# One more block by seven products in the last batch, and other PSUM banks for the last whole chunk's output

## The chip, the cores and the metric

The kernel runs on one core of a Trainium2 chip. The metric is the device time of one execution in microseconds (us), the median of several runs. The engines of the core have a queue of instructions each and run them strictly in their queue's order: TensorE (PE in the profile, with its weight loads as PEld), VectorE (DVE), ScalarE (ACT), GpSimd (POOL) and SyncE (SP, which issues DMAs). They wait for each other through semaphores. Matmuls write into PSUM, which holds eight banks of 128 partitions x 512 float32; VectorE and ScalarE read it from there.

## What is computed

For each of four batches, a cross-covariance attention over channels, then a multiplicative feed-forward network over all tokens:

```python
B, N, C = (4, 5824, 256)
qn = q / (np.linalg.norm(q, axis=1, keepdims=True) + 1e-06)
kn = k / (np.linalg.norm(k, axis=1, keepdims=True) + 1e-06)
s = kn.transpose(0, 2, 1) @ qn / tau
...
a = np.exp(s)
a /= a.sum(-1, keepdims=True) + 1e-09
x = v @ a                    # 23296 tokens x 256
a = x @ w1                   # w1, w2: 256 x 1024
b = x @ w2
h = a * b @ w3               # 1024 x 1024
return h @ w_out             # 1024 x 256
```

All inputs and the output are float32; the kernel multiplies in bfloat16 and adds up in float32.

## The kernel before

**What is multiplied.** The kernel never forms x. For each batch it folds the attention matrix into w1 and w2 (`Wf`), so that a and b come straight from v transposed (`vT`), and it multiplies w3 by w_out once (`W_sb`). A batch has 5824 tokens: eleven whole chunks of 512 (c = 0 to 10) and a small one of 192 columns (c = 11, 128 tokens and 64 left over). Each chunk has eight blocks of 128 hidden units (j = 0 to 7). For a block (c, j), `normal` (L988) runs two matmuls of 512 columns into a bank for a, ScalarE casts it to bf16 (`as`, L985), two more go into another bank for b, and VectorE multiplies the two into the staging tile `abh` (L1017, or L1013 into `left` for the small chunk).

**Blocks by seven.** In the last batch (b = 3) some blocks of two neighbouring chunks c and c + 1 are made together by a scheme of Strassen's kind, `by_seven` (L1028): seven matmuls of 512 columns in place of eight, on sums of tokens (`tsum`, made by POOL) and sums of weights (`wsum`). Its banks are X, Y, Z and T. The first X product is copied to Y by ScalarE (L1040), T is copied to SBUF (`t`, L1046), VectorE adds X and t into Z (L1051), X and t into `bs` (L1070), and makes the two products `abh` (L1075, L1082); ScalarE casts Y to `as`. X is used for four products, and the fourth waits until bs has been read from the third. So against two plain blocks, seven products cost ScalarE three copies in place of two, and VectorE four instructions in place of two. `BY_SEVEN` (L554) says how many blocks of each pair of chunks are made so; `plan` (L1387) spreads them evenly over the eight j by the formula (2 i + 1) 8 // (2 k) and places them among the plain ones. Up to two blocks by seven are under way at once, and their steps are mixed with those of plain blocks.

**Output.** When a chunk is whole, its output is made from `abh` and `W_sb`, mixed in between the blocks of later chunks. Most chunks go by `seven_products` (L758): products of 128 x 128 into prodA (bank out0), prodB and prodC (bank out1), on sums that POOL makes (`S`, L790 and L792, 2.1 us each) or, for chunks 4 and 6 of the last batch, by four accumulating DMAs that POOL issues (L800). Chunks 0, 2 and 9 of the last batch go plainly by `emit_half` (L1088): 32 matmuls of 256 columns, the first half into out0, the second into out1, each copied to the staging tile `osb` and stored from SP. Chunk 10, the last whole one, and the small chunk 11 go block by block as their blocks are made: `single` (L896) tells the planner when, and `emit_out` (L1117) issues the matmuls, 4 x 8 of 256 columns for chunk 10 into out0 and out1, 2 x 8 for chunk 11 into the banks G and out2. The last two blocks of chunk 11 are issued at the very end (`ends`).

**Banks.** Eight tags stand for the eight banks: ab0 to ab3, out0, out1 (which have one use at a time), G and out2. G and out2 hold scores and norms of the next batch while there is one. In the last batch (`spare`) they join ab0 to ab3 as a ring of six for the a, b, X, Y, Z and T tiles (`rings`, L575). A tag in the set `held` is not given out.

**What sets the order.** The kernel's order is written out by a planner that runs when the program is built: `now` and `free` keep estimated times of the engines and banks, and `step` (L1418) picks among the plain line, up to two lines by seven, and the output line the one that can go first by its estimate (the lambda that each line yields). POOL's sums are put in by `pool_due` by due times, and loads of v, q and k at moments of an agenda; ahead of each load, `gate` (L955) makes POOL copy one element of the last-made `abh` tile, so that POOL, which issues the load, waits for that instruction of VectorE. So a change to the blocks moves estimates, and with them the order on every engine, from the first block it touches on.

Of the kernel before, what the change touches and what calls it, by code (L numbers as in the profile page):

```python
# [32 lines left out]
def kernel(  # L33
# [14 lines left out]
    B, N, C = q.shape  # L48
# [16 lines left out]
    NCH = NT // 4 + 1  # L65
# [485 lines left out]
        )  # L551


    BY_SEVEN = {(3, 0): 3, (3, 2): 5, (3, 4): 4, (3, 6): 5, (3, 8): 4}  # L554
    PAIRED = {b: tuple(c for b2, c in sorted(BY_SEVEN) if b2 == b) for b in range(B)}
    PLAIN = {0: (0, ), 1: (), 2: (), 3: (0, 2, 9, )}
    BY_DMA = {3: (4, 6, )}
# [7 lines left out]
    FAR = 1e9  # L565
    base = [0.0]
    free = {}
    held = set()

    def work_on(engine, cost, *after):  # L570

        now[engine] = max(now[engine], *after, 0.0) + cost
        return now[engine] + LATE[engine]
# [146 lines left out]
    w_made = [FAR]  # L720
# [34 lines left out]
    def out_bank(tag, ready=0.0):  # L755
        return max(free.get(tag, 0.0), ready)
# [133 lines left out]
    def plain_products(b, c, ab2, whole):  # L890

        for i in range(FT):
            yield lambda i=i: max(out_bank(f"out{i // 4}", whole), w_made[0])
            emit_half(b, c, i, ab2)

    def single(b, c, j, ab, ready):  # L896

        yield lambda: max(
            ready, w_made[0], out_bank("out0"), out_bank("out1"), 0.0 if queued.get(b, 0) == NCH - 1 - b // (B - 1) else FAR
        )  # L900
        emit_out(b, c, j, ab)

# [12 lines left out]
    queued = {}  # L915
# [72 lines left out]
    def normal(b, c, j):  # L988
# [32 lines left out]
        if c == NCH - 1 and b == B - 1 and j >= FT - LAG_END:  # L1021
            ends.append(lambda only=None: emit_out(b, c, j, ab, only))
        elif c == NCH - 1 or (b == B - 1 and c == NCH - 2):
            put_out(b, c, single(b, c, j, ab, ready), 1)
# [63 lines left out]
    def emit_half(b, c, i, ab2):  # L1088

        h, jj = divmod(i, 4)  # L1090
        if i % 4 == 0:
            out_tiles[b, c, h] = psum.tile([P, 2, D], F32, tag=f"out{h}", name=f"o_{b}_{c}_{h}", bufs=1)
        if i == 0:
            out_tiles[b, c] = work.tile([P, 4, D], F32, tag="o_sb", name=f"osb_{b}_{c}", bufs=3)
        t, o = out_tiles[b, c, h], out_tiles[b, c]
        for j in (2 * jj, 2 * jj + 1):
            for k in range(2):
                nc.tensor.matmul(  # L1098
                    t[:, k, :], lhsT=ab2[j // 4][:, h, j % 4, k * P : (k + 1) * P], rhs=W_sb[:, j, :],
                    start=(j == 0 and k == 0), stop=(j == FT - 1), skip_group_check=True,  # L1100
                )
        work_on("PE", 4 * (D * MM_COL + MM_FIX))
        read = now["PE"] + LATE["PE"]
        if i == 3:
            nc.scalar.copy(o[:, 0:2, :], t)
            free["out0"] = work_on("ACT", 0.475, read)
        elif i == FT - 1:
            if b == B - 1:
                nc.scalar.copy(o[:, 2:4, :], t)
                free["out1"] = work_on("ACT", 0.475, read)  # L1110
            else:
                nc.vector.tensor_copy(o[:, 2:4, :], t)
                free["out1"] = work_on("DVE", 0.6, read)
            rows = out[b * N : b * N + NT * P, :].rearrange("(p i) c -> p i c", i=NT)
            nc.sync.dma_start(out=rows[:, 4 * c : 4 * c + 4, :], in_=o)

    def emit_out(b, c, j, ab, only=None):  # L1117

        small = c == NCH - 1
        if small:  # L1120
            lhs = [ab[:, :P]]
            if b % 2 == 1:
                lhs.append(lefts[b // 2][:, j, :, :].rearrange("p b t -> p (b t)")[:, P : P + 2 * LEFT])
        else:
            lhs = [ab[:, i // 2, i % 2 * P : (i % 2 + 1) * P] for i in range(4)]
        if j == 0:
            out_tiles[b, c] = [
                psum.tile([P, 2, D], F32, tag=tag, name=f"o_{b}_{c}_{tag}", bufs=1)
                for tag in ((("G", "out2") if b == B - 1 else ("out0", "out1"))[: len(lhs)] if small else ("out0", "out1"))
            ]  # L1130
        tl = out_tiles[b, c]
        for s, lhsT in reversed(list(enumerate(lhs))) if small and b == B - 1 else enumerate(lhs):
            if only is not None and s != only:
                continue
            h, o = (s, 0) if small else divmod(s, 2)
            nc.tensor.matmul(  # L1136
                tl[h][:, o, :], lhsT=lhsT, rhs=W_sb[:, j, :],
                start=(j == 0 and o == 0), stop=(j == FT - 1 and (small or o == 1)),
                skip_group_check=True,
            )  # L1140
        work_on("PE", len(lhs) * (D * MM_COL + MM_FIX))
        if j == FT - 1:
            read = now["PE"] + LATE["PE"]
            free["out0"] = work_on("ACT", 0.475, read)
            free["out1"] = work_on("DVE", 0.6, read)
            o = work.tile([P, 4, D], F32, tag="o_sb", name=f"osb_{b}_{c}", bufs=3)
            rows = out[b * N : b * N + NT * P, :].rearrange("(p i) c -> p i c", i=NT)
            if small:
                if b % 2 == 1 and only != 0:
                    o2 = work.tile([P, D], F32, tag="kr", name=f"oleft_{b}", bufs=1)  # L1150
                    nc.vector.tensor_copy(o2, tl[1][:, 0, :])
                    for m in (b - 1, b):
                        k = (m - b + 1) * LEFT
                        store = lambda m=m, k=k, queue=nc.sync: queue.dma_start(
                            out=out[m * N + NT * P : (m + 1) * N, :], in_=o2[k : k + LEFT, :]
                        )
                        if m < B - 1:
                            store()
                        else:
                            last_rows.append(store)  # L1160
                if only != 1:
                    nc.scalar.copy(o[:, 0, :], tl[0][:, 0, :])
                    other = nc.scalar if b == B - 1 else nc.sync
                    other.dma_start(out=rows[:, NT - 1, :], in_=o[:, 0, :])
                    if last_rows:
                        last_rows.pop()(queue=nc.scalar)
            else:
                nc.scalar.copy(o[:, 0:2, :], tl[0])
                nc.vector.tensor_copy(o[:, 2:4, :], tl[1])
                nc.sync.dma_start(out=rows[:, 4 * c : 4 * c + 4, :], in_=o)  # L1170
            if only is None:
                del out_tiles[b, c]
# [214 lines left out]
    def plan(b):  # L1387
# [6 lines left out]
        while c < NCH:  # L1394
            if c in PAIRED.get(b, ()):
                k = BY_SEVEN[b, c]
                mine = [(2 * i + 1) * FT // (2 * k) for i in range(k)]
# [119 lines left out]
```

## Time and profile before

| what | value |
|---|---|
| median of 3 runs | 550.82 us (550.64 to 550.88) |
| the profiled execution | 551.17 us |
| its span, first to last instruction | 549.1 us |
| granted TensorE clock, mean | 0.999 |
| DVE busy in the span | 425.0 us |
| ACT busy | 397.0 us |
| POOL busy | 416.1 us |
| a and b matmuls of 512 columns (L995) | 620 each, 184.4 us each |
| X matmuls on token sums (L980, two of a block's four) | 42, for 21 blocks |

The span is what the profile covers; about 2 us of the execution's time lie around it. The page names an instruction by its source line, engine, operation and tiles, written out<-in, and gives how many there are, their busy time and the mean duration. [...] Batch 3 takes the part of the span from about 436 us to the end: chunks 4 and 5 are made from about 463 to 481 us, chunks 6 and 7 to about 500, and chunk 10's output starts at 539.1.

In the timeline, a bracket behind a row gives how long the engine was idle before it and what ended that; in the chain of waits, "issue" is time in which an engine waited for nothing that the profile shows.

### The profile page before, as it was taken

How to read it: one execution, taken by the hardware profiler on the slowest of the kernel's cores; microseconds unless marked ns; L12 is line 12 of the kernel's file. 1: busy time of each engine (PE TensorE's matmuls, PEld its weight loads, DVE VectorE, ACT ScalarE, POOL GpSimd, SP SyncE). 2: the span in 40 equal slices, each digit the busy share in tenths (PEclk: the TensorE clock that was granted, in tenths of full speed). 3: DMA queues.
4: the chain of work that ended last, by engine and by line, in shares of the span. 5: the costliest groups of instructions: out<-in, count | busy, mean ns of one | idle time of the engine just before them, and what ended most of it. 6: DMA issues, size and time to landing. Idle time of an engine off the chain costs nothing.

```text
span 549.1 us, 12260 instructions
## 1 busy us (share of the span) xinstructions
PE 537.4 (98%) x4608; PEld 350.8 (64%) x4608; DVE 425.0 (77%) x748; ACT 397.0 (72%) x825; POOL 416.1 (76%) x343
## 2 busy tenths in 40 slices
PE   7799999999999999999999999999999999999996
PEld 4564566666677666666658666666667656666675
DVE  5477748999876888888766788888778788889861
ACT  5446648889777788888666888888778667677762
POOL 4270794979999499998996498979999846978560
PEclk9999999999999999999999999999999999999999
DMA  9999987995876849775582857776651334565513
GB/s 214 212 202 208 214 159 154 226 189 108 124 163 147 191 87 195 162 158 125 116 180 88 166 126 153 151 146 119 154 116 78 78 92 110 136 168 135 144 58 128
DMA packets 76747, 80.75 MB, mean 147 GB/s; under 512 B 54416, under 2 KB 59024, under 8 KB 76688
## 3 DMA queue, kind: packets, MB, share of 16 engines
q0 software_dynamic: 16816, 41.03, 42.7%
q1 hardware_dynamic: 59504, 38.22, 25.0%
q8 instruction: 36, 0.59, 0.4%
q10 hardware_dynamic: 368, 0.72, 0.4%
q14 instruction: 23, 0.19, 0.1%
HBM read 78.91 MB, written 23.86 MB: 187 GB/s over the span
## 4 chain that ended last, share of the span: by engine, by line
PE 92%; DMA 5%; DVE 1%; ACT 1%; issue 1%; POOL 0%; ACTq 0%; DVEq 0%; POOLq 0%
PE b L995 25%; PE a L995 25%; PE prodA L830 13%; PE prodC L830 6%; PE G L216 5%; PE prodB L830 3%; PE X L980 3%; DMA k<-in_k_dram 3%; PE o L1098 2%; PE fold L449 2%; DMA q<-in_q_dram 2%; PE o_out L1136 1%; PE w L1285 1%; PE Z L980 1%; PE Y L980 1%; PE T L980 1%
## 5 line engine op out<-in xcount | busy, mean ns | idle before, releaser
L1017 DVE TENSOR_TENSOR abh<-as,b 128x512 bf16<-128x512 bf16 x310 | 211.6, 684 | 68.7 <-ACT as L985 45.0
L985 ACT CAST as<-a 128x512 bf16<-128x512 f32 (+1 forms) x342 | 192.1, 563 | 70.0 <-PE a L995 57.4
L995 PE MATMUL a<-vT,Wf 128*128 128x512 bf16 x620 | 184.4, 379 | 0.1
L995 PE MATMUL b<-vT,Wf 128*128 128x512 bf16 x620 | 184.4, 379 | 0.0
L995 PEld LDWEIGHTS <-Wf 128*128 128x128 bf16 x1368 | 123.1, 98 | 77.7 <-issue 0.7
L790 POOL TENSOR_TENSOR S<-abh,abh 128x1024 bf16<-128x1024 bf16 x37 | 78.8, 2130 | 52.9 <-DVE abh L1017 34.7
L830 PEld LDWEIGHTS <-S 128*128 128x128 bf16 x1216 | 80.1, 98 | 22.9
L230 DVE TENSOR_TENSOR acc<-acc,sq 128x512 f32<-128x512 f32 x132 | 91.6, 694 | 1.2 <-ACT sq L213 0.3
L792 POOL TENSOR_TENSOR S<-S,abh 128x1024 bf16<-128x1024 bf16 x37 | 78.7, 2128 | 2.7
L792 POOL TENSOR_TENSOR S<-abh,S 128x1024 bf16<-128x1024 bf16 x37 | 79.4, 2147 | 0.1
L792 POOL TENSOR_TENSOR S<-abh 128x1024 bf16<-128x1024 bf16 x37 | 78.8, 2131 | 0.1
L830 PEld LDWEIGHTS <-abh 128*128 128x128 bf16 x968 | 64.1, 98 | 20.6 <-issue 0.8
L843 ACT COPY osb<-prodA 128x256 f32<-128x256 f32 x113 | 42.2, 373 | 16.3 <-PE prodA L830 15.7
L216 PE MATMUL G<-k,q 128*128 128x256 bf16 x276 | 52.4, 273 | 0.0
L216 PEld LDWEIGHTS <-q 128*128 128x128 bf16 x276 | 27.0, 98 | 32.1
L830 PE MATMUL prodA<-comb_T,S 128*128 128x128 bf16 x608 | 46.3, 219 | 0.0
L213 ACT ACTIVATE sq<-q 128x512 f32<-128x512 bf16 x69 | 43.8, 635 | 0.0
L213 ACT ACTIVATE sq<-k 128x512 f32<-128x512 bf16 x69 | 43.5, 630 | 0.0
L850 DVE TENSOR_TENSOR osb<-osb,prodC 128x256 f32<-128x256 f32 x76 | 31.4, 414 | 4.4 <-ACT osb L843 3.5
L130 POOL DMA_DIRECT2D q<-in_q_dram x27 | 15.2, 563 | 11.8 <-DMA q<-in_q_dram 5.7
L830 PE MATMUL prodB<-W_sb,abh 128*128 128x128 bf16 x312 | 23.8, 219 | 0.1
L830 PE MATMUL prodA<-W_sb,abh 128*128 128x128 bf16 x312 | 23.8, 219 | 0.0
(176 smaller groups left out, 642.9 us busy)
## 6 DMA issues: line engine op xcount, KB each, us to landing
out_dram<-osb SPq DMA_DIRECT2D x44, 512.0 KB, 3.4
k<-in_k_dram POOLq DMA_DIRECT2D x19, 512.0 KB, 8.0
v<-in_v_dram POOLq DMA_DIRECT2D x19, 512.0 KB, 6.9
q<-in_q_dram POOLq DMA_DIRECT2D x18, 512.0 KB, 5.5
w<-in_moe_w_dram POOLq DMA_DIRECT2D x4, 512.0 KB, 16.6
k<-in_k_dram POOLq DMA_DIRECT2D x4, 320.0 KB, 7.8
v<-in_v_dram POOLq DMA_DIRECT2D x4, 320.0 KB, 4.2
S<-abh SPq DMA_DIRECT2D x4, 256.0 KB, 3.0
```

The costliest lines, as they stand in the source:

```text
L213: nc.scalar.activation(out=sqs[0][:, :, part, :], in_=src[:, o : o + 2, :], func=AF.Square)
L216: nc.tensor.matmul(G[:, ct, :], lhsT=qt[:, i, ct * P : (ct + 1) * P], rhs=kt[:, i, :], start=(pr == 0 and part == 0 and ct == 0), stop=(pr ...
L230: nc.vector.tensor_add(accs[n], accs[n], sqs[0][:, part - 2])
L790: nc.gpsimd.tensor_add(x, a21, a22)
L792: nc.gpsimd.tensor_sub(x, *{2: (sums[1], a11), 3: (a11, a21)}.get(i) or (a12, sums[2]))
L830: nc.tensor.matmul(st[nm][:, i, :], lhsT=a[:, j, i * P : (i + 1) * P], rhs=w[j], start=(first and j == 0 and i == 0), stop=(j == 3), skip_ ...
L843: nc.scalar.copy(quarter(r, d), st[nm])
L850: nc.vector.tensor_add(quarter(r, d), quarter(r, d), st[nm])
L980: nc.tensor.matmul(dst, lhsT=lhsT, rhs=rhs, start=start, stop=True, skip_group_check=True)
L985: nc.scalar.copy(a_sb[:, :n], t[:, :n])
L995: nc.tensor.matmul(t[:, :n], lhsT=Wf[b][:, ct, w, j * P : (j + 1) * P], rhs=rhs_of(b, c, ct), start=(ct == 0), stop=(ct == CT - 1),)
L1017: nc.vector.tensor_mul(ab, two_halves(a_sb), two_halves(t))
```

## The change

```diff
-    BY_SEVEN = {(3, 0): 3, (3, 2): 5, (3, 4): 4, (3, 6): 5, (3, 8): 4}
+    BY_SEVEN = {(3, 0): 3, (3, 2): 5, (3, 4): 5, (3, 6): 5, (3, 8): 4}
...
+    def out_tags(b, c):
+        return ("G", "out2") if (b, c) == (B - 1, NCH - 2) else ("out0", "out1")
+
     def single(b, c, j, ab, ready):

         yield lambda: max(
-            ready, w_made[0], out_bank("out0"), out_bank("out1"), 0.0 if queued.get(b, 0) == NCH - 1 - b // (B - 1) else FAR
+            ready, w_made[0], *(out_bank(t) for t in out_tags(b, c)), 0.0 if queued.get(b, 0) == NCH - 1 - b // (B - 1) else FAR
         )
...
         if j == 0:
+            if b == B - 1 and not small:
+                held.update(("G", "out2"))
             out_tiles[b, c] = [
                 psum.tile([P, 2, D], F32, tag=tag, name=f"o_{b}_{c}_{tag}", bufs=1)
-                for tag in ((("G", "out2") if b == B - 1 else ("out0", "out1"))[: len(lhs)] if small else ("out0", "out1"))
+                for tag in out_tags(b, c)[: len(lhs) if small else 2]
             ]
```

The first edit makes five blocks of chunks 4 and 5 of the last batch by seven products in place of four: j = 0, 2, 4, 5 and 7, where it was 1, 3, 5 and 7. The second lets chunk 10's output of the last batch add up in G and out2, and the small chunk 11's in out0 and out1; from chunk 10's first output matmul on, G and out2 are held back from the ring. The planner's estimate for chunk 10's output looks at the new banks.

In the order of instructions that the changed program is built with, everything up to the last blocks of chunks 2 and 3 of the last batch (some 462 us into the span) is as before. In chunks 4 and 5 the blocks and the pieces of output among them are mixed in another order; some pieces of output of chunks 3 and 5 trade places with their neighbours; from the middle of chunks 6 and 7 on the order is the old one again up to the end of chunk 9's output. There, chunk 10's 32 output matmuls now come ahead of the pair a, b of block (11, 7), the last one, where they came behind it, and on ScalarE and VectorE the two copies of chunk 10's output come ahead of that block's cast and product. On POOL one instruction differs: the gate ahead of the load of v's last piece (chunks 10 and 11) copies from chunk 5's `abh` in place of chunk 4's, and waits for the product of the plain block (5, 6).

## The prediction

> **What bounds the kernel now.** I read the page first: PE is busy 98% of the span, and the chain that ended last is 92% PE. The clock row of its slices stays at full speed.
>
> ```profile
> span 549.1 us, 12260 instructions
> PE 537.4 (98%) x4608; PEld 350.8 (64%) x4608; DVE 425.0 (77%) x748; ACT 397.0 (72%) x825; POOL 416.1 (76%) x343
> PE 92%; DMA 5%; DVE 1%; ACT 1%; issue 1%; POOL 0%; ACTq 0%; DVEq 0%; POOLq 0%
> PEclk9999999999999999999999999999999999999999
> ```
>
> So in the steady part a matmul taken away shortens the program by its own length, unless another engine cannot follow. Next I read the timeline of the last batch, and looked on PE for starts that lie further apart than the width explains. A 512-column matmul follows the one before after 0.22 us, a 256-column one after 0.11. From 458 us on, PE waits noticeably at four places only: 487.1 (0.05 us), 498.4 (0.07), 515.4 (0.29) and 539.2 (0.29). The last is the one that the second edit touches, and the chain of waits shows it:
>
> ```profile
> 537.22 1.76 PE o L1098 x16
> 539.00 0.59 ACT osb L1109
> 539.59 0.04 issue
> 539.64 3.54 PE o_out L1136 x31
> ```
>
> PE finishes chunk 9 (L1098), runs the pair a, b of block (11, 7), starts chunk 10's output in bank out0, and then stands still until ScalarE has copied chunk 9's second half out of bank out1. The stages around the other edit come from the view of windows (columns: window, its length, then busy time and count of PE, PEld, DVE, ACT, POOL, then clock, DMA share, GB/s). Chunks 4 and 5 fill the first, with four blocks by seven; chunks 6 and 7 the second, with five:
>
> ```profile
> 466.00:482.00 16.00, 16.00 (x116) 9.73 (x114) 13.75 (x23) 11.12 (x22) 14.53 (x15) 1.00 0.59 149
> 482.00:499.00 17.00, 17.00 (x152) 10.55 (x150) 15.28 (x27) 12.75 (x29) 12.97 (x10) 1.00 0.63 134
> ```
>
> VectorE is the closest rival of PE: 86% busy with four blocks, 90% with five.
>
> **Part 1, one more block by seven.** Eight matmuls of 512 columns (a and b for two chunks, two halves each) become seven. That takes one matmul from PE, 0.22 us, and the rest of PE's list keeps its length. ScalarE gets one 512-wide copy more (three in place of two, 0.59 us each by L1046 and L1040, 0.48 apart), VectorE two more (Z and bs, 0.69 us each, 0.60 apart when queued, 1.2 us together). ScalarE is idle 4.9 us of the 16, so its copy costs nothing there. VectorE's 2.25 idle us shrink to about 1.0. Whether this is felt depends on order. The blocks are now j = 0, 2, 4, 5, 7 in place of 1, 3, 5, 7, so 0, 2, 4 and 5 come close together. I laid the new order of both queues over the rows from here:
>
> ```profile
> 467.81 0.38 PE L980 MATMUL X<-tsum,wsum 128*128 128x512 bf16 x1
> 468.47 0.68 DVE L1070 TENSOR_TENSOR bs<-X,t 128x512 bf16<-128x512 f32 x1
> 469.26 0.69 DVE L1075 TENSOR_TENSOR abh<-bs,Z 128x512 bf16<-128x512 bf16 x1
> ```
>
> The tightest place is the fourth product of block (4, 4), which needs X back from the bs add (L1070). From 467.81 to that product the new order has 26 matmuls of 512 columns and 24 of 256: 26 x 0.217 + 24 x 0.109 = 8.26, so PE wants it at 476.07. On VectorE, bs of block (4, 2) can start at 472.15, when its third X product is out; its product follows 0.79 later (469.26 - 468.47), then Z of (4, 4), two products and the bs add, at 0.60 each: the add starts at 475.34, ends at 476.03, and PE sees it at about 476.08. Slack is nil, so a VectorE that is a little late is paid in full. The cost lies between nothing and 1.2 us (both extra adds uncovered). The nearest rows are those of the stage that already has five blocks, with waits of 0.05 and 0.07; I take 0.05.
>
> **What moves with it.** POOL's gate ahead of the load of v's last piece named chunk 4's product; it now names the product for (5, 6). In the rows of before that instruction starts on VectorE at 481.75 and ends at 482.44, against 480.45 for the old one.
>
> ```profile
> 480.58 0.18 POOL L959 COPY gate_t<-abh 1x1 bf16<-1x1 bf16 x1 [0.66 <-DVE abh L1082]
> 481.64 0.56 POOL L130 DMA_DIRECT2D v<-in_v_dram  x1
> 483.93 2.11 POOL L790 TENSOR_TENSOR S<-abh,abh 128x1024 bf16<-128x1024 bf16 x1 [1.73 <-DVE abh L1075]
> 490.27 0.92 POOL L800 DMA_DIRECT2D S<-abh  x1
> 501.85 0.86 POOL L800 DMA_DIRECT2D abh<-S  x1
> 506.49 0.61 PE L830 MATMUL prodC<-W_sb,abh 128*128 128x128 bf16 x8
> ```
>
> The two loads move from 481.10 to about 483.1. POOL is through them at 484.2 and not at 482.2, so chunk 5's first sum starts some 0.3 us late; against a PE that is 0.2 ahead that is 0.5. Behind it in POOL's queue stand chunk 5's other sums, chunk 4's four accumulating transfers, the token sums for chunk 8, then chunk 7's sums. The last transfer of chunk 4 (abh<-S) is issued at 501.85 and takes 3.3 us to land, the median of the transfers into abh: 505.15, with its reader at 506.49. Slack 1.34, less 0.5 leaves 0.84. The transposes of the v piece on SP also move 1.9 us back, and chunk 3's store, queued behind them on SP, with them. The vT they write is first read after 516, and chunk 3's staging buffer is next written by chunk 7 after 505, so both are covered by over 10 us. But these transposes will now overlap the transfer issued at 490.27 for longer. Transfers into S took from 2.3 to 5.8 us to land, this one 4.2: the cost is 0 to 0.76 (1.6 late, less 0.84). I take 0.05, near its own row.
>
> **Part 2, the banks.** Chunk 10's output goes to G and out2, which the a, b blocks used. In the order of the changed kernel it waits for a product on VectorE and a cast on ScalarE for chunk 11's earlier blocks, rows that end before 538.2; chunk 9's last matmul is issued at 538.7. So it can start at 538.80 with no wait, ahead of pair (11, 7): 0.29 us saved. What then follows pair (11, 7)? With chunk 10's 32 matmuls at 538.80 (3.49), the pair runs at 542.29, chunk 11's output from 542.62, its product that needs block (11, 7) 13 x 0.109 later, at 544.04. Queued ahead of that block's cast on ScalarE and product on VectorE are now the two copies of chunk 10 (0.59 and 0.69 us by L1168 and L1169). VectorE's copy starts at 542.50 and lets go at 543.10; the cast runs 542.77 to 543.09, the product to 543.48. Half a microsecond is to spare. Afterwards everything moves by the same 0.29: the copies, the three last stores, their landing. Chunk 10's store is issued 0.6 earlier than now and clears the queues sooner, worth nothing to 0.1. The bounds are -0.39 and, if that half microsecond is missed by a 0.36 delay such as the one below, still -0.29, or 0 if a bank comes late; I take -0.29.
>
> Taking G and out2 away also leaves pair (11, 7) a ring of four banks. The rows of batches 0 to 2 run on four banks at a granted clock of 0.999 for the whole core.
>
> [...]
>
> **Sum.** -0.22 + 0.05 + 0.05 - 0.29 = -0.41. The profiled execution took 551.17 with a span of 549.1; its span becomes 548.7. The three runs have a median of 550.82, 0.35 under the profiled one, so the same difference gives 550.4.
>
> **The rivals.**
> *VectorE decides.* For it: nil slack at block (4, 4), and no easy stage between three stages of five blocks in which to catch up. Against it: the stage from 482 runs this way with 0.12 us of waits. Its price is a delay such as the one the chain shows at 514.83, where VectorE started an add 0.36 us after all that it is known to wait for: twice that, 0.72, undoes both gains: 550.82 - 0.51 + 0.72 = 551.0.
> *The transfers come late (slower).* If chunk 4's transfer from 490.27 lands 5.8 us after its issue, the next ones follow one after another and prodC at 506.49 waits 0.76: 550.82 - 0.46 + 0.76 = 551.1. It decides from a landing time of about 5.0, and the kernel is slower than before from about 5.5. For it: more overlap with the transposes. Against: of the twelve such transfers between 479 and 520 ten land in 4.2 or less, the others in 4.8 and 5.8.
> *The wait at 515.4 goes too.* It is made of this:
>
> ```profile
> 514.33 0.50 ACT t L1046
> 514.83 0.36 issue
> 515.18 0.71 DVE Z L1051
> ```
>
> A shift of POOL's transfers against PE may remove it: 550.4 - 0.29 = 550.1.
> *The second edit does nothing*, because copies of chunk 10 hold the last block up: 550.4 + 0.29 = 550.7.
>
> **How the numbers follow.** The forecast 0.52, VectorE 0.12, transfers 0.13, 515.4 gone 0.14, no gain from the banks 0.09. The likeliest value is 550.4, its own range 550.2 to 550.65. From 549.95 to 551.05 I leave out the far ends of the transfer case and a double gain. A change of 0.2%, 1.1 us here, is about what a measurement of this kernel can tell from no change; nearly every case lies inside. Faster by more needs over twice the counted gain (0.05, all of it cases not seen); slower by more needs a new wait of 1.6 us, the transfers' far end or one not seen (0.09).
>
> **What would show it.** Right: no osb copy in the chain ahead of chunk 10's output, whose matmuls come ahead of pair (11, 7); 618 matmuls of 512 columns in place of 620 each for a and b; one Z and one bs more (L1051, L1070 in the numbering of before); the v load near 483. Wrong: a PE start over 0.2 us late between 470 and 482 behind bs or Z; prodA or prodC of chunk 4 waiting for a DMA between 500 and 507; an idle PE ahead of the last eight output matmuls.

## The result, and the profile after

The changed kernel takes 550.12 us, the median of 22 runs (549.92 to 550.47), against 550.88 of 22 runs of the kernel before (550.53 to 551.10). The ratio is 0.9987, with a 95% interval of 0.9981 to 0.9993: 0.76 us less, within 0.2% of before. The forecast was 550.4, in a range of 549.95 to 551.05. The range holds the time, the forecast's own narrower one (550.2 to 550.65) does not: the gain is nearly twice the 0.41 that the forecast added up, and the time is that of the rival "the wait at 515.4 goes too" (550.1). So the question is whether that rival came true, and through what.

The page of the changed kernel, its span, busy times, chain and clock:

```profile
span 548.1 us, 12254 instructions
PE 536.1 (98%) x4599; PEld 350.5 (64%) x4607; DVE 426.5 (78%) x750; ACT 397.4 (73%) x826; POOL 416.0 (76%) x343
PE 92%; DMA 5%; issue 1%; ACT 1%; DVE 1%; POOL 0%; DVEq 0%; POOLq 0%
PEclk9999999999999999999999999999999999999999
```

PE still sets the time (98% busy), at a mean granted clock of 1.000. The profiled execution took 550.1 us. VectorE has two instructions more, which the groups show to be one Z and one bs, 22 in place of 21:

```profile
L998 PE MATMUL a<-vT,Wf 128*128 128x512 bf16 x616 | 183.2, 379 | 0.2
L1054 DVE TENSOR_TENSOR Z<-X,t 128x512 f32<-128x512 f32 x22 | 15.3, 695 | 1.6 <-ACT t L1049 0.9 <-ACT osb L843 0.7
L1073 DVE TENSOR_TENSOR bs<-X,t 128x512 bf16<-128x512 f32 x22 | 15.1, 686 | 1.6 <-PE X L983 1.3
```

(Eight matmul records are missing from this trace, 4,599 beside 4,607 weight loads, so x616 stands for the 618 that were expected. In the changed kernel's listing most lines of these functions have numbers three higher than before.)

Spans can't be subtracted as they stand: the two profiled executions differ by 0.30 us before the last batch begins, all of it ahead of 145 us, where the change touches nothing. So I count from the first X of batch 3, the first matmul of a block by seven (429.26 before, 428.96 after; the batch's blocks begin here, some 7 us ahead of the 436 named above), and list what PE lost on the way: the distance between two starts less what the width explains (a 512-column matmul is shown with 379 ns, and the next one starts 0.22 us after it). The two profiled executions of the kernel before and the three of the changed one agree to 0.02 us in it.

| | before | after |
|---|---|---|
| first X of batch 3 to chunk 9's last matmul | 109.43 | 108.98 |
| from there to the last matmul | 5.85 | 5.57 |
| last matmul's start to the last landing | 3.44 | 3.43 |
| waits on PE near 446, 457 | 0.25, 0.05 | 0.25, 0.05 |
| near 465, 475, 479 | - | 0.02, 0.02, 0.08 |
| near 487, 498 | 0.05, 0.07 | -, 0.02 |
| near 515 | 0.29 | - |
| near 518 | - | 0.05 |
| ahead of chunk 10's output (539) | 0.29 | - |

The sum of the parts: one matmul less, -0.22; the wait at 515, -0.29; the other waits ahead of 539, from 0.42 to 0.49, +0.07; the wait at 539, -0.28. Together -0.72, and -0.73 is what the first two rows show.

The end, in the chain of waits (start, length, engine, tile, line, count):

```profile
536.46 1.75 PE o L1101 x16
538.21 0.22 PE o_G L1141 x2
538.43 0.22 PE o_out L1141 x2
...
541.70 0.16 PE a L998 x2
541.87 0.17 PE b L998 x2
542.03 0.30 PE o_out L1141 x3
```

Chunk 10's output starts straight behind chunk 9's last matmul, in G and an out bank by turns, and the pair of block (11, 7) follows it. No copy stands in between, as one did before.

The stage of chunks 4 and 5, in the timeline (start, length, engine, line, operation):

```profile
475.04 0.68 DVE L1073 TENSOR_TENSOR bs<-X,t 128x512 bf16<-128x512 f32 x1
475.77 0.38 PE L983 MATMUL X<-tsum,Wf 128*128 128x512 bf16 x1
...
477.71 0.63 ACT L988 CAST as<-a 128x512 bf16<-128x512 f32 x1
478.37 0.69 DVE L1020 TENSOR_TENSOR abh<-as,b 128x512 bf16<-128x512 bf16 x1 [0.62 <-ACT as L988]
479.11 0.38 PE L998 MATMUL a<-vT,Wf 128*128 128x512 bf16 x1
```

The fourth product of block (4, 4) starts 0.05 us after the bs add that it needs ends at 475.72, 0.02 late: the slack there was nil, as the prediction had worked out. The larger loss is one that it did not see. The matmul at 479.11 (a of block (5, 6)) waits for the bank that the product of block (4, 6) at 478.37 empties, and that product waits for a cast that stands fifth in a row on ScalarE, from 475.79 on without a gap. The first two of the five are Y and t of block (4, 5), which the new order puts right behind block (4, 4).

The transfers, from POOL's timeline and the reader from PE's:

```profile
483.47 0.56 POOL L130 DMA_DIRECT2D v<-in_v_dram  x1
484.06 2.13 POOL L790 TENSOR_TENSOR S<-abh,abh 128x1024 bf16<-128x1024 bf16 x1
490.42 0.92 POOL L800 DMA_DIRECT2D S<-abh  x1
501.31 0.85 POOL L800 DMA_DIRECT2D abh<-S  x1
505.95 0.61 PE L830 MATMUL prodC<-W_sb,abh 128*128 128x128 bf16 x8
```

The v loads moved to 482.9 and 483.5 (predicted 483.1). The transfer from 490.42 landed at 493.89, 3.5 us later, and the last one at 504.59, 1.36 ahead of its reader. Nothing waits for a transfer here.

And 515, in the chain:

```profile
514.42 0.43 PE b L998 x2
514.86 0.43 PE a L998 x2
515.29 0.22 PE X L983
515.50 0.22 PE Z L983
```

PE passes the place where it had stood 0.29 us without a stop. VectorE's Z of block (8, 5) starts at 514.32, 0.04 us after the end of the copy t that it waits for, where it was 0.36 before:

```profile
514.32 0.70 DVE L1054 TENSOR_TENSOR Z<-X,t 128x512 f32<-128x512 f32 x1 [0.61 <-ACT t L1049]
```

### The profile page after: what moved, and what is told of

The parts are those of the page before. It is cut to its first block, busy times and chain, and to the rows that moved or that the text cites. A ratio compares the mean times of both kernels' runs of the same rounds, so it can differ in the third digit from the quotient of the medians.

```text
span 548.1 us, 12254 instructions
## 1 busy us (share of the span) xinstructions
PE 536.1 (98%) x4599; PEld 350.5 (64%) x4607; DVE 426.5 (78%) x750; ACT 397.4 (73%) x826; POOL 416.0 (76%) x343
## 4 chain that ended last, share of the span: by engine, by line
PE 92%; DMA 5%; issue 1%; ACT 1%; DVE 1%; POOL 0%; DVEq 0%; POOLq 0%
PE a L998 25%; PE b L998 25%; PE prodA L830 13%; PE prodC L830 6%; PE G L216 6%; PE X L983 3%; PE prodB L830 3%; DMA k<-in_k_dram 3%; PE o L1101 3%; PE fold L449 2%; DMA q<-in_q_dram 2%; PE w L1290 1%; PE o_out L1141 1%; PE Y L983 1%; PE Z L983 1%; PE T L983 1%
```

## The experiments

### The two edits alone, and both kernels again

Four runs on one chip, with the kernel before at 550.78 us (33 runs). First the block alone:

```diff
-    BY_SEVEN = {(3, 0): 3, (3, 2): 5, (3, 4): 4, (3, 6): 5, (3, 8): 4}
+    BY_SEVEN = {(3, 0): 3, (3, 2): 5, (3, 4): 5, (3, 6): 5, (3, 8): 4}
```

> The first edit alone: five blocks of chunks 4 and 5 by seven, chunk 10's output in out0 and out1 as before. Theory A (the parts add up as the prediction has them, and the 0.29 us wait of PE near 515 belongs to the executions that show it, not to the order): 0.15 to 0.25 us faster than before, from the one matmul less; the 0.29 wait before chunk 10's output is still there. Theory B (the new order also removes the wait near 515, which is part of the old order): 0.4 to 0.5 us faster, and no start of Z on VectorE over 0.3 us late near 515. Theory C (VectorE eats the gain): 0.1 faster to 0.5 slower, with PE starts late behind bs or Z between 470 and 482.

The banks alone:

```diff
+    def out_tags(b, c):
+        return ("G", "out2") if (b, c) == (B - 1, NCH - 2) else ("out0", "out1")
...
+            if b == B - 1 and not small:
+                held.update(("G", "out2"))
...
-                for tag in ((("G", "out2") if b == B - 1 else ("out0", "out1"))[: len(lhs)] if small else ("out0", "out1"))
+                for tag in out_tags(b, c)[: len(lhs) if small else 2]
```

> The second edit alone: four blocks of chunks 4 and 5 by seven as before, chunk 10's output in G and out2. Theory A and B: 0.25 to 0.35 us faster than before, the copy of chunk 9's second half no longer in the chain of waits. Theory D (the banks give more than the wait, because chunk 10's store leaves earlier and the last stores land sooner): 0.4 to 0.6 us faster, with the time from the last matmul to the last landing at least 0.1 shorter than before's 3.4 us.

The kernel before, unchanged:

> The kernel before, unchanged, for a second profile and as a control of the timing: a ratio of 1 within 0.1%. Theory A: PE's wait near 515 (0.29 us behind a Z on VectorE that starts 0.36 late) is absent or elsewhere, while the waits at 446 (0.25) and 539 (0.29) recur. Theory B: it recurs at the same instruction with 0.2 to 0.4 us.

The changed kernel, unchanged:

> The changed kernel, unchanged, for a second profile and in the same rounds as its parts: 0.6 to 0.9 us faster than before, and the sum of the two parts within 0.15 us if they are independent. Theory A: some wait of 0.2 to 0.4 us may show up at any late VectorE start in this profile, the first profile having had none near 515. Theory B: none near 515 again.

| | median us | ratio, 95% interval | first X to chunk 9's last | to the last matmul | wait near 515 |
|---|---|---|---|---|---|
| block alone | 550.26 | 0.9991, 0.9982 to 1.0000 | 108.98 | 5.85 | none |
| banks alone | 550.32 | 0.9991, 0.9983 to 1.0000 | 109.46 | 5.57 | 0.30 |
| before again | 550.71 | 0.9998, 0.9990 to 1.0007 | 109.44 | 5.85 | 0.29 |
| after again | 550.13 | 0.9989, 0.9980 to 0.9998 | 108.97 | 5.57 | none |

The parts add up by the starts of PE: the block gives 0.45, and the banks 0.28 at the end, where they act. The medians agree, though each of the two intervals reaches 1.0000. From the last matmul to the last landing it is 3.43 to 3.44 us in all four, so the earlier store of chunk 10 is worth nothing (theory D falls). And the wait at 515 belongs to the order of the blocks. It is in the three profiles of the old order, with the new banks too, and in none of the three of the new one (theory B holds, A falls). The chain of the kernel with the banks alone:

```profile
514.02 0.50 ACT t L1049
514.52 0.38 issue
514.90 0.71 DVE Z L1054
```

That left open what in the new order removes it. POOL's transfers, which the prediction had named, were an unlikely answer by now: the transfer that POOL issues beside it (abh<-abh) stands in both kernels at the same distance from the end of t, 513.82 against 514.83 before and 513.32 against 514.3 after. So I looked for other starts on VectorE and ScalarE that come later than the last instruction waited for and than the end of the one ahead. In the profile of before, from 90 us on, there are five that are over 0.1 us late in this sense. Then I counted their places in the instruction lists that the compiler writes, semaphore-only instructions included (an engine's rows in the trace, counted in order of time, give the same numbers). The last column is the time from the end of the semaphore-only instruction ahead to the start:

| engine | number | number modulo 128 | start us | late by us | behind the semaphore us |
|---|---|---|---|---|---|
| VectorE | 192 | 64 | 98.75 | 0.25 | 0.40 |
| VectorE | 576 | 64 | 249.59 | 0.44 | 0.40 |
| VectorE | 960 | 64 | 410.94 | 0.15 | 0.41 |
| VectorE | 1216 | 64 | 515.18 | 0.36 | 0.40 |
| ScalarE | 832 | 64 | 411.82 | 0.36 | 0.32 |

All five stand at 64 modulo 128, and each right behind a semaphore-only instruction. Elsewhere an instruction that has nothing else to wait for starts 0.04 us behind such a one, on both engines. So the uneven delays are one delay, 0.4 us from the semaphore to the start on VectorE, of which the work that the engine is still doing hides a part. The page of before has queues that carry instructions (queue, kind, packets, MB, share of 16 engines):

```profile
q8 instruction: 36, 0.59, 0.4%
q14 instruction: 23, 0.19, 0.1%
```

The trace holds 12,260 rows, 9,225 of them PE's; if q8's 36 packets carry PE's list, 0.59 MB over 9,225 is 64 bytes an instruction. Each packet of q8 has 16,384 bytes, which by this estimate is 256 instructions, and each of q14 in the span 8,192, which is 128. The packets' times are in the trace too. For each of the 19 places at which VectorE and ScalarE pass 64 modulo 128, a packet of q14 begins, from 0.5 us ahead of the start there to 3.7 us behind it; at the five late starts it begins 0.64 to 3.67 us behind. I read this as such a list asking there for its next 128 instructions; for the late instruction that packet comes too late to be what it waits for. In the new order Z of block (8, 5) has number 1219. The next runs put this to the test.

### One place later, three places earlier, and a later transfer

Three runs on one chip, with a fourth that follows below; the kernel before was at 550.74 us (34 runs).

```diff
     nc.vector.memset(eps_t, 1e-6)
+    pad = consts.tile([P, 1], F32)
+    nc.vector.memset(pad, 0.0)
```

> The kernel before, with one more VectorE instruction at the very start (a memset of 128 words that nothing reads), which moves every later VectorE instruction by one place in its list. In the list of before, with the semaphore-only instructions counted, the late Z of block (8, 5) is number 1216 and stands right behind a semaphore wait; the other late starts that nothing in the trace explains are numbers 192, 576 and 960 on VectorE and 832 on ScalarE, all 64 more than a multiple of 128. Theory P (place in the list): Z is number 1217 now, the semaphore wait ahead of it 1216, and what happens at 1216 goes on while that semaphore is waited for; the wait on PE at 515.4 (0.29 us) is gone, from batch 3's first X to the last PE start it takes 115.05 us in place of 115.28, and the kernel is 0.2 to 0.3 us faster than before. The late starts near 98.7, 249.6 and 410.9 go as well, without effect on PE. Theory T (POOL's transfers, as the prediction had it) and theory O (the order of the products): nothing of either is touched, so the wait at 515.4 stays at 0.28 to 0.29 and the time is that of before within 0.1.

The changed kernel, with three instructions of the start taken from VectorE's list:

```diff
-    nc.vector.memset(ones_b, 1.0)
...
-    nc.vector.memset(tiny, 1e-9)
...
-    nc.vector.memset(eps_t, 1e-6)
...
         load_piece("q", 0, pi)
+    nc.gpsimd.memset(ones_b, 1.0)
+    nc.gpsimd.memset(tiny, 1e-9)
+    nc.gpsimd.memset(eps_t, 1e-6)
     load_piece("k", 0, 4)
```

> The changed kernel, with three memsets of the start moved from VectorE to POOL, so that every later VectorE instruction stands three places earlier and Z of block (8, 5) is number 1216, right behind a semaphore wait, as it was in the kernel before. The order of all else, and the transfers, are those of the changed kernel. Theory P: Z starts about 0.36 us late again and PE waits 0.25 to 0.30 us near 514.6; from batch 3's first X to the last PE start 114.80 in place of 114.55; 550.35 to 550.45 against 550.12 of the changed kernel, so 0.35 to 0.45 below before. Theories T and O: no wait there, 550.1 to 550.2.

The kernel before, with POOL held up ahead of one transfer:

```diff
+                if c == 6 and i == 1:
+                    nc.gpsimd.memset(warm, 0.0)
                 nc.gpsimd.dma_start(out=dst, in_=src, accum_op=ALU.add)
```

> The kernel before, with one POOL memset of 128x512 put ahead of the accumulating transfer that POOL issues at 513.82 (1.18 us, chunk 6's sum into abh), so that this transfer is issued 0.2 to 0.7 us later against PE and VectorE. Theory T: the late start of Z at 515.18 goes, or moves by the same amount as the end of the issue (at 515.00 before), so that the PE wait of 0.29 changes by at least 0.15 one way or the other. Theory P: the VectorE list is unchanged, Z stays 0.36 late and PE waits 0.28 to 0.30; time as before within 0.1 unless the later transfer itself is waited for.

| | median us | ratio, 95% interval | first X to the last matmul | Z's number | wait near 515 |
|---|---|---|---|---|---|
| before, one place later | 550.40 | 0.9995, 0.9987 to 1.0004 | 115.09 | 1217 | none |
| after, three places earlier | 550.39 | 0.9996, 0.9987 to 1.0005 | 114.77 | 1216 | 0.29 |
| before, later transfer | 550.94 | 1.0010, 0.9996 to 1.0025 | 115.31 | 1216 | 0.30 |

(The kernel before has 115.28 and the changed one 114.55. All three intervals take in 1, so it is the traces that decide here and not the medians. One of the 12 runs with the later transfer took 555.90; the trace is of another.) One memset of 128 words that nothing reads takes the wait out of the old order. Its chain at that place:

```profile
514.48 0.43 PE b L997 x2
514.91 0.43 PE a L997 x2
515.34 0.21 PE X L982
```

and Z in its timeline:

```profile
514.37 0.70 DVE L1053 TENSOR_TENSOR Z<-X,t 128x512 f32<-128x512 f32 x1 [0.61 <-ACT t L1048]
```

Three instructions fewer in VectorE's list bring it back in the new order of the blocks:

```profile
513.76 0.50 ACT t L1046
514.25 0.36 issue
514.61 0.71 DVE Z L1051
```

And with POOL's issue moved 0.5 us back against the other engines, Z is as late as it was, and starts in the middle of that issue. From the two timelines of this run:

```profile
513.74 0.83 POOL L801 MEMSET warm<- 128x512 bf16 x1
514.21 1.18 POOL L802 DMA_DIRECT2D abh<-abh  x1
...
515.14 0.70 DVE L1053 TENSOR_TENSOR Z<-X,t 128x512 f32<-128x512 f32 x1 [0.96 <-ACT t L1048]
```

Theories T (transfers) and O (order of the products) both fall, and P (place in the list) holds in all three. The other late starts go with the numbers as well. With one more memset, those near 98.7, 249.6 and 410.9 are gone, and ScalarE's at its number 832, whose list is untouched, stays. VectorE's numbers 704 and 832, which now stand right behind a semaphore-only instruction, start 0.40 us after it, and so does number 704 with three instructions fewer. Where VectorE still has work when the number comes up, nothing is late: numbers 320, 832 and 1088 of the old list start 0.09 us ahead of the end of the instruction before, and behind the semaphore-only number 704 the next one starts 0.08 us ahead of it. Number 448 is semaphore-only too, and begins 0.40 us behind the semaphore-only one ahead of it.

### More blocks by seven

The first was run with the three above, the others on one chip with the kernel before at 550.79 us (15 runs). All change one line of the changed kernel:

```diff
-    BY_SEVEN = {(3, 0): 3, (3, 2): 5, (3, 4): 5, (3, 6): 5, (3, 8): 4}
+    BY_SEVEN = {(3, 0): 3, (3, 2): 5, (3, 4): 5, (3, 6): 5, (3, 8): 5}
```

> The changed kernel with 23 blocks by seven products: chunks 8 and 9 take five as chunks 4 and 5 do since the change. One matmul of 512 columns less, 0.22 us. If VectorE can follow as it did at chunk 4 (0.0 net there, waits of 0.02 and 0.085 in place of two of 0.05): 549.9 against 550.12 of the changed kernel, and from batch 3's first X to the last PE start 114.3. If VectorE, which now has six stages of chunks without an easy one, decides: waits near Z and the bs adds after 500 us that add 0.3 or more, 550.2 to 550.6. By theory P one VectorE instruction at number 1216 may be late as well; the one there is a join of an output half (osb), for which PE does not wait at once, so nothing is expected of it.

```diff
-    BY_SEVEN = {(3, 0): 3, (3, 2): 5, (3, 4): 5, (3, 6): 5, (3, 8): 4}
+    BY_SEVEN = {(3, 0): 4, (3, 2): 5, (3, 4): 5, (3, 6): 5, (3, 8): 4}
```

> The changed kernel with the extra block by seven in chunks 0 and 1 (four in place of three), 23 in all. One matmul of 512 columns less, 0.22 us, if VectorE follows: 549.9. The stage of chunks 0 and 1 stands right after the last batch's weights, with one wait of 0.25 on PE in it already (446 us) and the order of both chunks differs throughout. If VectorE decides there, waits of 0.3 or more before 458, and 550.2 to 550.6. By the place in VectorE's list nothing is late near 515: number 1216 is a semaphore wait with work queued ahead of it.

With both, (3, 0): 4 and (3, 8): 5:

> The changed kernel with four blocks in chunks 0 and 1 and five in chunks 8 and 9, 24 by seven in all: two matmuls of 512 columns less, 0.43 us. If both stages can be followed, 549.6 to 549.7 against 550.12 of the changed kernel and 549.8 of the version with five in chunks 8 and 9 alone. If VectorE decides in the stage of chunks 0 and 1 but not later, the same step is lost here as in the version with four there alone, and the two versions differ from those without it by the same amount.

The changed kernel beside them:

> The changed kernel again, on the same chip and in the same rounds as the two others, so that their differences from it can be read directly: 550.1, from batch 3's first X to the last PE start 114.55, no wait on PE near 515, Z of block (8, 5) on time (number 1219 in VectorE's list). Anything else would mean that the place in the list isn't what decides.

| | median us | ratio to before, 95% interval | first X to the last matmul |
|---|---|---|---|
| five in chunks 8 and 9 | 549.79 | 0.9982, 0.9973 to 0.9991 | 114.34 |
| four in chunks 0 and 1 | 556.18 (4 runs) | 1.0100, 1.0085 to 1.0115 | 120.42 |
| both | 556.44 (4 runs) | 1.0099, 1.0084 to 1.0114 | 121.64 |
| changed kernel again | 550.01 | 0.9987, 0.9978 to 0.9996 | 114.53 |

Five blocks in chunks 8 and 9 give what one matmul is worth once more, 0.20 of 0.22 between the marks, and VectorE follows: PE has no wait over 0.06 us after 500. The median is below the changed kernel's 550.01 to 550.13 too, though the two were not run in the same rounds.

Four blocks in chunks 0 and 1 cost 5.9 us, where the expectation's dearest case had 0.5. In the main it isn't VectorE. In the chain PE waits twice for the same kind of transfer:

```profile
497.14 5.45 DMA abh<-abh
502.59 0.05 issue
502.64 0.62 PE prodC L830 x8
...
518.60 5.46 DMA abh<-abh
524.06 0.05 issue
524.11 0.62 PE prodC L830 x8
```

They cost 2.68 and 1.72 us, 4.4 of the 5.9; the rest is in smaller waits, of at most 0.44 each, from 439 us on. The first can be followed against the changed kernel, counted from the first X. There this transfer is issued at 66.88, lands 3.35 later and is read at 71.99, a slack of 1.76. With the new order it is issued 1.21 later, takes 2.10 longer (the next transfer, issued 2.2 us behind it, overlaps it), and its reader comes 1.08 earlier: 1.76 - 1.21 - 2.10 - 1.08 = -2.63. One more block in that stage reorders both chunks' blocks and all that the planner puts behind them. This is the prediction's slower rival, in another of chunk 4's transfers than the one that it watched.

Beside five blocks in chunks 8 and 9, four in chunks 0 and 1 cost 7.30 us (121.64 less 114.34), beside four there 5.89 (120.42 less 114.53). A part of the difference is the clock. In the windows of this run (window, its length, busy time and count of PE, PEld, DVE, ACT, POOL, then clock, DMA share, GB/s):

```profile
499.70:503.00 3.30, 0.49 (x4) 0.06 (x2) 1.38 (x2) 0.69 (x2) 3.22 (x4) 0.94 0.93 161
503.00:506.00 3.00, 3.00 (x20) 2.17 (x21) 0.94 (x2) 0.58 (x1) 1.85 (x2) 0.50 0.02 3
506.00:509.00 3.00, 3.00 (x26) 1.70 (x23) 2.13 (x5) 2.19 (x5) 0.00 (x0) 1.00 0.00 0
```

The same transfer lands 0.3 us later here, PE waits 2.97 us for it in place of 2.68, and then it runs at a granted clock of 0.50 until 506.0, with the T and X matmuls starting 0.43 us apart in place of 0.22, which costs half of some 3.0 us, an estimated 1.5. After the wait of 2.68 in the other kernel the clock stays at 1.00. The spell seems to go with the execution more than with the kernel: mean clocks of 0.995 or 0.996 stand beside three of the four runs here and beside one of the four of the other kernel, and the medians differ by 0.26 only. From there on the waits of the two kernels differ, so what VectorE does in chunks 8 and 9 can't be judged from this run.

## Why the prediction was right, and where it was wrong

**The block, -0.22: right.** One matmul of 512 columns went. The 0.45 of the run with the block alone is this, the wait at 515.4 (0.29) and the next point (0.07 the other way), with 0.01 for the roundings.

**VectorE, +0.05: right in size, in part by luck.** The nil slack at block (4, 4) cost 0.02, as it was worked out. New waits of 0.02, 0.02, 0.08 and 0.05 replace two of 0.05 each, +0.07 in the sum above. The largest goes back to ScalarE's queue: the step "ScalarE is idle 4.9 us of the 16, so its copy costs nothing there" took a mean over a stage for the state of a queue. Copies of a block by seven stand directly ahead of the casts there. The rival "VectorE decides" (551.0) did not come.

**POOL and the transfers, +0.05: nothing.** The loads moved by 1.8 us, where 1.9 were worked out, the transfers landed in 3.3 to 3.5 us, and of the slack that was put at 0.84 there was 1.36. The rival "transfers late" didn't come here, but with four blocks in chunks 0 and 1 it did: landing in 5.45 us, a transfer decided by itself.

**The banks, -0.29: right.** From chunk 9's last matmul to the last one it is 5.85 us in every run without this edit and 5.57 in every one with it, in the order that was worked out. VectorE's copy and its product for the last block run from 541.74 to 542.72, a little sooner against the pair than expected, and no matmul waits for them. Four banks for the last pair were no burden: the granted clock is 1.00 from 536.0 to 545.5, beyond the last matmul. Chunk 10's earlier store is worth nothing.

**The wait at 515.4, the term that was left out.** The forecast counted it at nothing and gave its end a chance of 0.14, through "a shift of POOL's transfers against PE". That is the step that failed, in size and in cause: -0.29 was missing from the sum, and -0.41 - 0.29 = -0.70 is what came (-0.73 by the starts of PE, -0.76 in the medians). The range held the time because it reached far enough down to take in that rival, whose reason was wrong. The runs show that the cause is the place of one add in VectorE's instruction list: late at number 1216 in both orders, on time at 1217 and 1219. What was needed to see it stood in the profile of before. The changed order puts two more adds and a semaphore-only instruction ahead of that Z, which moves it from 1216 to 1219, and four other late starts at 64 modulo 128 were there to be counted. With that the likeliest value would have been 550.82 - 0.70 = 550.1.

What stays open is what takes the time at these numbers. A packet of q14 begins within 3.7 us of each, and the late instructions start 0.64 to 3.67 us ahead of theirs; that the packet brings the next 128 instructions, and that asking for it is what costs the 0.4 us, is a reading that no run here tests. What is measured is that the instruction at the number is late when it stands right behind a semaphore-only one and the engine runs out of work within the 0.4 us: in the kernel before VectorE lost 0.15 to 0.44 us at a time, and ScalarE 0.36 once.

## What to carry to other kernels

A start that comes some tenths of a microsecond after everything it waited for, the same in every execution, is worth a count of its place in the engine's list: if such starts share a remainder, one idle instruction at the head of the list (or one fewer) can be tried. Here one memset took a wait of 0.29 us off PE, and three instructions fewer brought one of 0.29 back. Any edit that adds or removes instructions on such an engine shifts all later ones, so that a gain or loss of a few tenths of a microsecond far from the edit may be no effect of it at all. And an engine's mean idle share in a stage doesn't cover an added instruction (ScalarE was idle for 4.9 us of 16 in the kernel before, and with one copy more PE lost 0.08 behind its queue): what counts is who stands behind it in the queue.

## What was not expected of the hardware

The instructions found late in the traces here stand at numbers 64 modulo 128 of their lists, right behind a semaphore-only one. They start 0.40 to 0.43 us after it on VectorE and 0.32 on ScalarE, where 0.04 is usual; in the kernel before, five had nothing later to wait for and an engine without work to cover it, and lost 0.15 to 0.44 us. One added memset of 0.06 us early in VectorE's list made the kernel before 0.19 us shorter between the marks (115.28 to 115.09), and 0.34 in the medians of 11 and 34 runs, whose interval takes in no change. Accumulating transfers of the same size and kind (256 KB, abh into abh) landed 3.35 and 4.29 us after their issue in the changed kernel, where the next one followed 5.5 us later, and 5.45 and 5.46 with four blocks in chunks 0 and 1, where it followed after 2.2 and 3.3 us. That the overlap is the reason was not tried by itself, and it can't be all: one took 4.83 in the kernel before, with the next 5.9 us behind it. And a wait of 2.97 us on PE was followed by 3.0 us of work at a granted clock of 0.50, one of 2.68 us by full clock. The length of the idle stretch alone doesn't explain it here: by the trace's clock records the fall came 2.4 us into one of 2.8, and the other was 2.5 long without a fall.
